# A program laid out step by step in one order, with one window geometry for all batches, in an attention and MoE kernel

## The chip, the cores and the metric

The kernel runs on one NeuronCore of a Trainium2 chip. Five engines work side by side, each through its own queue in program order: TensorE (PE) for matmuls, VectorE (DVE), ScalarE (ACT), GpSimd (POOL), and SyncE (SP), which only issues transfers. Transfers between HBM and on-chip memory (SBUF) run on the core's 16 DMA engines, whichever queue issued them. Matmul results go to PSUM, eight banks of 512 fp32 values on each of 128 partitions.

The metric is the device time of one execution in microseconds (us), as the median of several runs. Beside it stands one execution under the hardware profiler, with a time of its own, on which all readings of the trace rest.

## The reference

Two stages follow each other. The first is attention with B, H, S, D = 8, 8, 576, 64, as a sum of a coarse part (queries, keys and values averaged over groups of four tokens) and a local part (each query sees the keys less than four positions away):

```python
q_d, k_d, v_d = (x.reshape(B, H, S // 4, 4, D).mean(axis=3) for x in (q, k, v))
out_up = np.repeat(softmax(scale * q_d @ k_d.T) @ v_d, 4, axis=2)
mask = np.abs(pos[:, None] - pos[None, :]) < 4
out_local = softmax(np.where(mask, scale * q @ k.T, -1e9)) @ v
x = (out_up + out_local).transpose(0, 2, 1, 3).reshape(4608, 512)
```

The second is two dense layers on the 4608 tokens, with ELU between them:

```python
h = x @ w_in                                    # 512 -> 2048
g = np.where(h > 0, h, np.exp(np.minimum(h, 0)) - 1)
out = g @ w_out                                 # 2048 -> 512
```

## The kernel before

All matmuls take fp16 operands. The tokens of the dense layers are cut into nine blocks `t` of 512. A block's first layer (`mm1`, line 720) is 16 steps of four 128x512 matmuls, its second layer (`mm2`, line 740) 16 steps of four. Block 0 has its first layer cut into halves of 256 tokens (`mm1_part`, line 699), so that it can start on the first half. Between the layers each step has an exponential on ACT (line 724) and two DVE operations (lines 725 and 726).

Attention is done per batch `b` and pair of heads `j` (0 to 3); a batch gives 576 tokens, so block `t` needs batches up to about `t`. For a pair the steps are:

- **load**: `load_qk` and `load_v` on SP. For batches 0 and 1 (but the first pair) q and k are loaded by `load_cast` on POOL's queue, which converts to fp16 on the way. q and k lie as six tokens a partition on 96 partitions, two heads side by side. v comes as rows of 256 bytes.
- **cast**: `cast_qk`, `cast_v` on POOL, to fp16.
- **transposes** on PE (lines 324 and 329) into PSUM, and copies out (lines 359 and 366). From batch 3 on, k is turned by a transposing DMA (`flip`).
- **sums**: groups of four tokens, for q on POOL (lines 395, 397), for k on DVE (line 378).
- **scores** (lines 459, 472), exponentials on ACT (line 482), the mask on DVE (line 497), all in ten windows of 58 queries and 64 keys.
- **denominators** (line 519) of all four pairs and their reciprocals, spread over the partitions by matmuls and copies (lines 582, 592) for batches 0 to 2, and through DRAM (`spread_out`, `spread_in`) from batch 3 on.
- **outputs** (lines 603, 623), `normalise` on DVE (lines 667, 672), and the sum of both parts into the dense layers' input `xt` (line 684), nearly all on POOL.

Batch 0 has a geometry of its own: windows of 96 queries and 112 keys, a mask that is added by matmuls (line 423), sums of four tokens by matmuls (lines 340, 346), and outputs in two halves of the tokens. `keep` (line 759) are matmuls on zeros in the front that keep PE active.

The order is set by a time that is given to each step: `at(time, fn, *args)` collects the events, and they are emitted sorted by that time. The times stand in tables for the front (`F`), for batches 1 to 3 (`PLAN`), for later ones (`LATER`, `LAST`), and as straight lines for the matmuls of the dense layers (`MM1`, `MM2`). The tables put the loads of `w_in` (`load_wi`, line 172, four loads of 512 columns into one tile `WI`) behind the loads and casts of batch 0's v. PSUM tiles come from pools with turning buffers: two or three of two banks for transposes, scores and outputs, two of one bank for `hp`, two for the rest.

Of the kernel before, what the change touches and what calls it, by code (L numbers as in the profile page):

```python
# [19 lines left out]
QB, KW, NB, PAD = 96, 112, 6, 8  # L20
HB = 3 * QB
TPP = S // QB
# [5 lines left out]
RW = S + SD  # L28
KG, CG = 96, 24
# [6 lines left out]
I1 = 31  # L36


def _np_consts():

    f16 = np.float16
    off = np.arange(KW) - PAD
    m = np.zeros((KW, NB, QB), dtype=f16)
    for c in range(NB):
        for u in range(QB):
            ok = (np.abs(off - u) < 4) & (off + QB * c >= 0) & (off + QB * c < S)
            m[ok, c, u] = 1.0
    m = m.reshape(KW, S)
    neg = ((m - 1) * 30000).astype(f16)
    rs = np.zeros((QB, 3, SD), dtype=f16)  # L50
    for c in range(3):
        rs[np.arange(QB), c, (TPP * np.arange(QB) + 2 * c) // 4] = 0.25
    vr = np.zeros((KW, 32), dtype=f16)
    vr[PAD + np.arange(QB), np.arange(QB) // 4] = 0.25
    ind = np.zeros((KW, 190), dtype=f16)
    ind[:, I1] = 1.0
    ind[np.arange(KW) % 32 < CG, 63 + I1] = 1.0
    ind[:, 126:] = 1.0
    for n, z in enumerate((10, 5)):
        ind[:, 127 + 32 * n : 126 + 32 * n + z] = 0.0  # L60
    return np.eye(KW, dtype=f16), neg, rs.reshape(QB, 3 * SD), vr, ind


def _np_windows():
# [26 lines left out]
    return mask.reshape(128, WL), vr.reshape(128, 96), ind  # L91
# [12 lines left out]
def kernel(  # L104
# [11 lines left out]
    dr = ctx.enter_context(tc.tile_pool(name="dr", bufs=1, space=bass.MemoryType.DRAM))  # L116
    ctx.enter_context(nc.allow_low_precision("fp16 operands of TensorE"))
    ctx.enter_context(tc.manual_schedule())

    def const(a, name, queue):  # L120
        t = C[name] = sb.tile(list(a.shape), FP16, tag=name, bufs=1, name=name)
        queue.dma_start(out=t[:], in_=nc.inline_tensor(a, name=name + "c").ap())

    front = ctx.enter_context(ExitStack())
    ps = ctx.enter_context(tc.tile_pool(name="ps", bufs=1, space=bass.MemoryType.PSUM))
    fp = front.enter_context(tc.tile_pool(name="fp", bufs=1, space=bass.MemoryType.PSUM))
    late = {}

    def one(name, dt=FP32):
        return ps.tile([128, 512 if dt == FP32 else 1024], dt, tag="misc", bufs=2, name=name)  # L130

    turns = [0, 1, 2]

    def two(name, dt=FP32):

        turns.append(turns.pop(0))
        pool = fp if turns[-1] == 2 else ps
        return pool.tile([128, 1024 if dt == FP32 else 2048], dt, tag=f"two{turns[-1]}", bufs=1, name=name)

    def bank(tag, name):  # L140
        pool = late["ps"] if tag == "hp" else ps
        return pool.tile([128, 512], FP32, tag=tag, bufs=2, name=name)

    def close_front():
        front.close()
        turns.remove(2)
        late["ps"] = ctx.enter_context(
            tc.tile_pool(name="late", bufs=1, space=bass.MemoryType.PSUM)
        )

    def g2(ap, a, n):

        return _free(ap[:, a : a + 1], [[512, 2], [1, n]])
# [3 lines left out]

    id_np, neg_np, sums_np, vr_np, ind_np = _np_consts()
    mask_np, vr2_np, ind2_np = _np_windows()
    C = {}  # L160
    WI = sb.tile([128, DMC, DFF], FP16, tag="WI", bufs=1, name="WI")
    WO = sb.tile([128, FCN, DM], FP16, tag="WO", bufs=1, name="WO")
    KT = [sb.tile([128, S + 2 * KO], FP16, tag=f"kt{i}", bufs=1, name="kt") for i in range(4)]

    def w_in(dc, fc):

        a = 512 * (fc // 4) + fc % 4
        return WI[:, dc, a : a + 509 : 4]

    def load_wi(a, z):  # L170
        src = moe_w_in.rearrange("(c p) m -> p c m", p=128)[:, :, a:z]
        nc.gpsimd.dma_start(out=WI[:, :, a:z], in_=src)

    def load_wo(n):
        src = moe_w_out[512 * n : 512 * n + 512].rearrange("(p c) m -> p c m", c=4)
        nc.gpsimd.dma_start(out=WO[:, 4 * n : 4 * n + 4, :], in_=src)

    KD = [sb.tile([128, 2 * KG + 16], FP16, tag=f"kd{i}", bufs=1, name="kd") for i in range(4)]
    KE = [sb.tile([128, 192], FP16, tag=f"ke{i}", bufs=1, name="ke") for i in range(4)]
    QT = [sb.tile([128, S + 4], FP16, tag=f"qt{i}", bufs=1, name="qt") for i in range(4)]  # L180
    qk32, qk16, v32s, v16s = {}, {}, {}, {}
    st = {}

    def runs_of(src, b, j):

        a = src[b, 2 * j]
        return bass.AP(
            tensor=a.tensor, offset=a.offset, ap=[[TPP * D, QB], [S * D, 2], [1, TPP * D]]
        )

    def by_head(x):

        return x[:].rearrange("p c e d -> p (c e d)").rearrange("p (e n) -> p e n", e=2)

    def is_cast(b, j):

        return b < 2 and (b, j) != (0, 0)

    def load_cast(b, j):
        qk16[(b, j)] = []  # L200
        for src, name in ((q, "q16"), (k, "k16")):
            x = sb.tile([QB, NB, 2, D], FP16, tag=name, bufs=4, name=name)
            nc.gpsimd.dma_start(out=by_head(x), in_=runs_of(src, b, j))
            qk16[(b, j)].append(x)

    def load_qk(b, j, held=False):

        got = []
        for src, name in ((q, "q"), (k, "k")):
            a = src[b, 2 * j]  # L210
            t = sb.tile([QB, 2 * NB, D], FP32, tag=name + "32", bufs=3, name=name + "32")
            if held:
                nc.vector.memset(t[0:1, 0, 0:1], 0.0)
            runs_ = name == "q" or b < FLIP
            nc.sync.dma_start(
                out=t[:].rearrange("p (e r) d -> p e (r d)", e=2) if runs_ else t[:],
                in_=bass.AP(
                    tensor=a.tensor, offset=a.offset,
                    ap=[[TPP * D, QB], [S * D, 2], [1, TPP * D]] if runs_
                    else [[D, QB], [QB * D, 2 * NB], [1, D]],  # L220
                ),
            )
            got.append(t)
        qk32[(b, j)] = got

    AP_ = sb.tile([1, 1], FP16, tag="apart", bufs=1, name="apart")

    def apart(x):

        nc.gpsimd.tensor_copy(out=AP_[:], in_=x)  # L230

    def cast_qk(b, j, half=False):

        got = []
        for t, name in list(zip(qk32.pop((b, j)), ("q16", "k16")))[:: 1 if b < FLIP else -1]:
            x = sb.tile([QB, NB, 2, D], FP16, tag=name, bufs=4, name=name)
            src = t[:].rearrange("p (e c) d -> p c e d", e=2)
            if half:
                act(out=x[:, :, 0, :], in_=src[:, :, 0, :])
                dve(out=x[:, :, 1, :], in_=src[:, :, 1, :])  # L240
            else:
                nc.gpsimd.tensor_copy(out=x[:], in_=src)  # L242
                apart(x[0:1, 0, 0, 0:1])
            got.append(x)
        qk16[(b, j)] = got[:: 1 if b < FLIP else -1]

    V00 = sb.tile([KW, 2 * NB, D], FP32, tag="v32", bufs=3, name="v32")

    def load_v(b, j):

        a = v[b, 2 * j]
        if b:
            load_windows(b, j, a)
            return
        t = V00 if (b, j) == (0, 0) else sb.tile([KW, 2 * NB, D], FP32, tag="v32", bufs=3, name="v32")

        def part(p0, p1, i0, i1):
            nc.sync.dma_start(
                out=t[p0:p1, i0:i1, :],
                in_=bass.AP(  # L260
                    tensor=a.tensor, offset=a.offset + (QB * i0 - PAD + p0) * D,
                    ap=[[D, p1 - p0], [QB * D, i1 - i0], [1, D]],
                ),
            )

        if (b, j) == (0, 0):
            part(0, KW, 1, 2 * NB)
            part(PAD, KW, 0, 1)
        else:
            part(0, KW, 0, 2 * NB)  # L270
        v32s[(b, j)] = t

    def load_windows(b, j, a):

        t = sb.tile([128, 2 * WM, D], FP32, tag="v32", bufs=3, name="v32")
        if b == 1:
            nc.vector.memset(t[0:1, 1, 0:1], 0.0)

        def part(h, e, n=64, m0=0, m1=WM):
            nc.sync.dma_start(  # L280
                out=t[64 * h : 64 * h + n, WM * e + m0 : WM * e + m1, :],
                in_=bass.AP(
                    tensor=a.tensor, offset=a.offset + (WQ * h - 3 + S * e + 2 * WQ * m0) * D,
                    ap=[[D, n], [2 * WQ * D, m1 - m0], [1, D]],
                ),
            )
# [760 lines left out]
```

## Time and profile before

| | us |
|---|---|
| median of 3 runs | 352.03 (350.53 to 354.69) |
| span of the profiled execution | 355.1 |
| PE / DVE / ACT / POOL busy in it | 336.1 / 236.4 / 180.3 / 160.8 |
| `mm2` matmuls (line 740), 592 | 147.0 |
| `mm1` matmuls (line 720), 512 | 133.4 |
| `mm1` matmuls of block 0 (line 699), 128 of half the width | 17.3 |

How to read it: the span runs from the first to the last instruction. The busy time of an engine is the time in which at least one of its instructions ran; matmuls are pipelined, so one of them shows some 380 ns of its own while the next starts 216 ns after it. "PEclk" is the share of full speed that TensorE's clock was granted. A chain of waits lists, in order of time, the pieces of work that released each other up to the last instruction. Of DMA traffic the profile shows, by queue, packets, bytes, and the time that they took as a share of the 16 engines: q0 is what POOL issues, q1 what SP issues.

### The profile page before, as it was taken

The page shows a single profiled execution, that of the slowest core. Times are in us where ns is not written, and L with a number is a line of the kernel's source. Part 1 is how long each engine was busy: PE and PEld are TensorE (multiplying, and loading weights), DVE is VectorE, ACT ScalarE, POOL GpSimd, SP SyncE. Part 2 cuts the span into 40 slices and gives each one's busy share as a digit, 9 for nine tenths or more (in the row PEclk, how much of TensorE's full clock was granted, in tenths as well). Part 3 has the DMA queues.
Part 4 walks back from the last instruction along what each step waited for, and adds up shares of the span by engine and source line. Part 5 has one row for each costly group of instructions (what it writes and reads, how often), then busy time and mean ns, then how long its engine had stood idle before and what let it go on. Part 6 is the DMA issues. An engine that isn't in the chain of part 4 may idle for free.

```text
span 355.1 us, 10487 instructions
## 1 busy us (share of the span) xinstructions
PE 336.1 (95%) x4288; PEld 185.5 (52%) x4288; DVE 236.4 (67%) x466; ACT 180.3 (51%) x312; POOL 160.8 (45%) x298
## 2 busy tenths in 40 slices
PE   7993998799979999999999999999999999999996
PEld 3762885344545454545454555555455544444443
DVE  2334799566789877987697789768755855555510
ACT  4580587225755664466456645663553444444421
POOL 4464449279495834974397449855300500000000
PEclk9998799959999999999999999999999999999999
DMA  8999979997999698998979796943004010011012
GB/s 173 184 166 203 191 172 216 215 186 185 189 152 224 120 205 168 167 185 174 181 155 206 158 218 144 188 123 61 30 32 118 31 59 30 31 46 43 31 59 89
DMA packets 100304, 48.89 MB, mean 138 GB/s; under 512 B 81617, under 2 KB 95265, under 8 KB 100257
## 3 DMA queue, kind: packets, MB, share of 16 engines
q1 hardware_dynamic: 94417, 41.86, 57.8%
q0 software_dynamic: 5600, 6.26, 10.8%
q8 instruction: 33, 0.54, 0.7%
q10 hardware_dynamic: 240, 0.11, 0.2%
q14 instruction: 14, 0.11, 0.1%
HBM read 41.97 MB, written 9.55 MB: 145 GB/s over the span
## 4 chain that ended last, share of the span: by engine, by line
PE 72%; DMA 13%; DVE 6%; ACT 3%; issue 2%; POOL 2%; SPq 1%; DVEq 0%; POOLq 0%; ACTq 0%
PE op L740 31%; PE hp L720 28%; DMA v<-in_v_dram 6%; DMA rcb<-rd 3%; DMA WO<-in_moe_w_out_dram 3%; DVE ln L672 2%; PE sc L759 2%; PE tqk L329 2%; DMA rd<-rc 2%; PE lg L603 2%; DVE e L725 1%; PE sc L459 1%; ACT e L724 1%; DVE gt L726 1%; PE lg L623 1%
## 5 line engine op out<-in xcount | busy, mean ns | idle before, releaser
L740 PE MATMUL op<-WO,gt 128*128 128x512 f16 (+2 forms) x592 | 147.0, 377 | 1.0 <-DVE gt L726 0.6
L724 ACT ACTIVATE e<-hp 128x512 f16<-128x512 f32 x144 | 86.1, 599 | 110.5 <-PE hp L720 95.7
L720 PE MATMUL hp<-xt,WI 128*128 128x512 f16 x512 | 133.4, 384 | 0.7 <-DVE gt L726 0.5
L726 DVE SCALAR_TENSOR_TENSOR gt<-hp,e 128x512 f16<-128x512 f32 x144 | 99.6, 692 | 6.4
L725 DVE TENSOR_SCALAR e<-e 128x512 f16<-128x512 f16 x144 | 60.7, 421 | 58.1 <-ACT e L724 57.6
L740 PEld LDWEIGHTS <-gt 128*128 128x128 f16 x592 | 55.6, 98 | 62.8 <-issue 3.0
L720 PEld LDWEIGHTS <-WI 128*128 128x128 f16 x512 | 55.5, 115 | 49.6 <-issue 3.1
L684 POOL TENSOR_TENSOR xt<-ln 128x128 f16<-128x128 f16 (+7 forms) x55 | 36.7, 695 | 50.8 <-DVE ln L672 50.8
L482 ACT ACTIVATE pex<-sc 128x580 f16<-128x580 f32 (+1 forms) x56 | 30.2, 596 | 9.7 <-PE sc L472 9.7
L395 POOL TENSOR_TENSOR t<-qt 128x288 f32<-128x288 f16 x27 | 18.1, 671 | 36.8 <-ACT qt L359 36.8
L303 POOL CAST v<-v 128x640 f16<-128x640 f32 (+1 forms) x32 | 24.2, 756 | 21.1 <-DMA v<-in_v_dram 21.0
L746 ACT COPY os<-op 128x512 f32<-128x512 f32 (+2 forms) x37 | 21.4, 577 | 19.3 <-PE op L740 19.1
L378 DVE TENSOR_REDUCE ke<-kt 128x145 f16<-128x580 f16 x28 | 21.0, 751 | 2.4 <-ACT kt L366 2.4
L359 ACT COPY qt<-tqk 128x576 f16<-128x576 f16 x28 | 17.9, 638 | 8.5 <-PE tqk L329 6.7
L699 PE MATMUL hp<-xt,WI 128*128 128x256 f16 x128 | 17.3, 288 | 4.6 <-issue 4.6
L672 DVE TENSOR_TENSOR ln<-lg,rcb 128x580 f16<-128x580 f32 x28 | 21.1, 752 | 0.0
L242 POOL CAST q<-q 96x768 f16<-96x768 f32 x24 | 19.9, 828 | 0.0
L242 POOL CAST k<-k 96x768 f16<-96x768 f32 x24 | 19.8, 825 | 0.1
L699 PEld LDWEIGHTS <-WI 128*128 128x128 f16 x128 | 13.6, 118 | 5.8 <-issue 4.7
L497 DVE TENSOR_TENSOR pex<-pex,MASK 128x580 f16<-128x580 f16 x28 | 14.0, 500 | 3.8 <-ACT pex L482 3.6
L397 POOL TENSOR_TENSOR qd<-t 128x144 f16<-128x144 f32 x27 | 12.4, 461 | 2.1
L459 PEld LDWEIGHTS <-kt 64*64 64x64 f16 x560 | 7.0, 108 | 11.7 <-issue 8.8
(113 smaller groups left out, 271.6 us busy)
## 6 DMA issues: line engine op xcount, KB each, us to landing
out_dram<-os SPq DMA_DIRECT2D x35, 256.0 KB, 2.2
v<-in_v_dram SPq DMA_DIRECT2D x111, 80.0 KB, 4.6
q<-in_q_dram SPq DMA_DIRECT2D x25, 288.0 KB, 4.1
k<-in_k_dram SPq DMA_DIRECT2D x25, 288.0 KB, 5.1
rcb<-rd SPq DMA_DIRECT2D x10, 364.0 KB, 4.6
WI<-in_moe_w_in_dram POOLq DMA_DIRECT2D x4, 512.0 KB, 10.9
WO<-in_moe_w_out_dram POOLq DMA_DIRECT2D x4, 512.0 KB, 9.2
q<-in_q_dram POOLq DMA_DIRECT2D x7, 144.0 KB, 7.2
```

Source lines behind the costliest of these rows:

```text
L242: nc.gpsimd.tensor_copy(out=x[:], in_=src)
L303: nc.gpsimd.tensor_copy(out=v16[:], in_=v32[:].rearrange("p (e c) d -> p c e d", e=2))
L482: nc.scalar.activation(out=s["p"][:, :, a : a + n], in_=g2(sc, a, n), func=AF.Exp, scale=SCALE / 16 if a else SCALE,)
L672: nc.vector.tensor_tensor(out=ln[:, 0 : 2 * WL].rearrange("p (m h u) -> p m h u", h=2, u=WQ), in0=_free(lg[:, 0:1], [[WQ, WM], [512, 2], [ ...
L684: eng.tensor_tensor(out=xt(t)[:, j, t0 - TBLK * t : t1 - TBLK * t], in0=ln[:, a:z], in1=_rep4(ln[:, ga : ga + (z - a) // 4]), op=AB.add,)
L699: nc.tensor.matmul(FS[i][:, 256 * f : 256 * f + 256], w_in(dc, 2 * n + f), xts[0][:, dc, 256 * h : 256 * h + 256], start=(f == dc == 0), s ...
L720: nc.tensor.matmul(hp, w_in(dc, fc), xts[t][:, dc, :], start=(dc == 0), stop=(dc == DMC - 1),)
L724: nc.scalar.activation(out=e, in_=hp, func=AF.Exp)
L725: nc.vector.tensor_scalar(out=e, in0=e, scalar1=1.0, scalar2=-1.0, op0=AB.min, op1=AB.add)
L726: nc.vector.scalar_tensor_tensor(out=to, in0=hp, scalar=0.0, op0=AB.max, in1=e, op1=AB.add)
L740: nc.tensor.matmul(op_[:, a:z], gts[t][:, fc, 128 * tt : 128 * tt + 128], WO[:, fc, a:z], start=(fc == 0), stop=(fc == FCN - 1),)
L746: nc.scalar.copy(out=os_[:, a:z], in_=op_[:, a:z])
```

## The change

The program is written anew.

- **One geometry.** Batch 0 uses the windows of the later batches. Its mask, sums and token halves of its own go, and so do their constants (`NEG`, `R`, `SEL` and three more loads); what is left comes in one load, `con`.
- **Nine tokens a partition.** q and k are loaded as 9 tokens of one head on each of 128 partitions (rows of 2304 bytes; before: 1536). One transpose turns 64 partitions and 64 columns of one head, so a tensor takes 18 small transposes, two at a time in opposite corners of the array; before it was 6 or 12. From batch 3 on, k is loaded and turned by DMA as before.
- **Sums of four** are two additions of halves for q and k alike, each given to DVE or POOL.
- **PSUM by name.** Eight banks in four pairs; each step names its bank.
- **Whole blocks.** Block 0's first layer is made of 512-wide matmuls like the others. `WI` is two tiles, each loaded in two halves.
- **An order.** Each step is a word, `name.numbers`, the last number often the engine (0 ACT, 1 DVE, 2 POOL, 4 SP) or the bank; the words are carried out as they stand. Many steps get another engine than before: 44 of 64 `ad` (the sum into `xt`) are on DVE, 32 of 64 `s` on DVE, 12 of 82 casts on DVE and 6 on ACT, 10 of 144 `em` on POOL. Output pieces of the last 128 rows (384 and 128 columns) are interleaved, and the 128 columns are stored first.

The order up to the end of batch 0 reads as follows (`lx` load of q or k, `lv` load of v, `wi` load of `w_in`, `cx`/`cv` casts, `t` transposes, `e` copy out, `s` sums, `sc` scores, `x` exponentials, `mk` mask, `vs`/`vc` coarse v, `dn`/`rc` denominators, `sp`/`sy` spreading, `ne`/`fa` outputs, `n` normalise, `m` first layer, `w` second layer, `hv`/`hx` a write that holds a load back):

```diff
+ORDER = """
+id.0 zeros.0.1 lx.0.0.1.2 lx.0.0.0.4 zeros.2.1 warm.12.7 con.0 lx.1.0.0.4 lx.1.0.1.2 zeros.3.1 lv.0.0.1.4
+lx.0.0.3.2 zeros.1.1 lv.0.0.2.4 lx.0.0.2.2 lv.0.0.3.4 lx.1.0.3.2 lv.0.2.0.4 lx.1.0.2.2 lv.0.2.1.4 four.0.1
+wi.0.0.2 four.1.1 wi.0.1.2 lv.0.2.2.4 wi.1.0.2 cx.0.0.0.0 lv.0.2.3.4 t.0.0.1.4 t.0.0.0.5 lv.0.0.0.4
+e.0.0.1.4.0 wi.1.1.2 cx.1.0.0.1 e.0.0.0.5.0 s.0.0.1.1 lv.0.1.0.4 warm.2.7 t.1.0.1.6 t.1.0.0.7 s.0.0.0.1
+lv.0.1.1.4 e.1.0.1.6.0 lx.0.1.0.2 e.1.0.0.7.0 lv.0.1.2.4 s.1.0.1.1 warm.2.5 t.0.0.3.4 lv.0.1.3.4 s.1.0.0.1
+sc.0.1.0 e.0.0.3.4.0 lv.0.3.0.4 lx.1.1.0.2 sc.0.0.1 x.0.0.1.0 lv.0.3.1.4 s.0.0.3.1 warm.1.7 t.0.0.2.5
+x.0.0.0.1 mk.0.1.1 lv.0.3.2.4 e.0.0.2.5.0 mk.0.0.1 cv.0.2.2 lv.0.3.3.4 x.1.0.1.0 s.0.0.2.1 warm.6.7 t.1.0.3.6
+x.1.0.0.1 cv.0.0.2 vs.0.2.7 e.1.0.3.6.0 dn.0.0.2.4 lx.0.1.1.2 vs.0.0.5 s.1.0.3.1 lx.1.1.1.2 warm.2.3 t.1.0.2.6
+rc.0.0.2.4 sc.0.3.0 e.1.0.2.6.0 cv.0.1.1 sp.0.0.1 x.0.0.3.0 s.1.0.2.1 warm.1.4 vs.0.1.5 x.1.0.3.0 mk.0.3.1
+vc.0.0.5.0 warm.2.6 sc.0.2.0 sy.0.0.1.0 sp.0.1.2 x.0.0.2.0 ne.0.0.1 cv.0.3.1 lx.0.1.2.2 fa.0.0.1 x.1.0.2.0
+mk.0.2.1 warm.1.6 vs.0.3.7 sy.0.1.2.0 n.0.0.1 dn.0.2.4.6 vc.0.1.7.0 ne.0.1.0 hv.1.0.1 hv.1.1.1 hv.1.2.1
+hv.1.3.1 fa.0.1.0 lv.1.0.0.4 rc.0.2.4.6 ad.0.0.0.2 lv.1.0.1.4 n.0.1.0 warm.3.5 sp.0.2.2 lx.1.1.2.2 lv.1.0.2.4
+sp.0.3.1 ad.0.0.1.1 m.0.0.0.1.7 sy.0.2.2.0 lv.1.0.3.4 ad.0.1.0.1 ad.0.1.1.2 m.0.1.0.1.6 sy.0.3.1.0 lv.1.2.0.4
+m.0.0.1.2.7 ne.0.2.0 fa.0.2.0 lv.1.2.1.4 m.0.1.1.2.6 ne.0.3.1 n.0.2.0 lx.0.1.3.2 lv.1.2.2.4 fa.0.3.1
+lv.1.2.3.4 n.0.3.1 ad.0.2.0.2 lv.1.1.0.4 ad.0.2.1.1 lv.1.1.1.4 ad.0.3.0.1 ad.0.3.1.2 warm.15.5 m.0.0.2.3.7
...
+w.8.3.12.16.0.384.7 w.8.3.12.16.384.512.4 r.8.3.0.384.7.0 r.8.3.384.512.4.1 st.8.3.384.512 st.8.3.0.384
+"""
```

and the code that carries it out:

```diff
+    PB = [ps.tile([128, 1024], FP32, tag=f"pb{i}", bufs=1, name=f"pb{i}") for i in range(4)]
+    def bank(n):
+        return PB[n // 2][:, 512 * (n % 2) : 512 * (n % 2) + 512]
...
+    def load_x(x, b, j, eng):
+        a = (q, k)[x][b, 2 * j]
+        src = bass.AP(tensor=a.tensor, offset=a.offset, ap=[[NINE * D, 128], [1, NINE * D]])
+        if is_cast(b, j):
+            queues[eng].dma_start(out=nth((Q16, K16)[x], b, j)[:, 0:S], in_=src)
+            return
...
+    def load_wi(n, i, eng):
+        src = moe_w_in.rearrange("(c p) m -> p c m", p=128)
+        queues[eng].dma_start(
+            out=WI[n][:, 2 * i : 2 * i + 2, :], in_=src[:, 2 * i : 2 * i + 2, 1024 * n : 1024 * n + 1024]
+        )
...
+    def turn(x, b, j, p):
+        src, to = nth((Q16, K16)[x], b, j), bank(p).bitcast(FP16)
+        for c in range(NINE):
             for e in range(2):
+                r = heads(e)
+                nc.tensor.transpose(to[r, 64 * c : 64 * c + 64], src[r, 64 * c : 64 * c + 64], ID[r, r])
...
+    def sums(x, b, j, eng):
+        if x == 0:
+            src, n, to = QT[j][:, 0:S], SD, QD[j][:]
+        else:
+            src, n = KT[j][:, KO : KO + 2 * WL], 2 * WL // 4
+            to = KE[j][:, 0 : 32 * WM].rearrange("p (c u) -> p c u", u=32)[:, :, 0:WG]
+        t2 = T2[eng - 1][:, 0 : 2 * n]
+        at = src.rearrange("p (g f) -> p f g", f=2)
+        engines[eng].tensor_tensor(out=t2, in0=at[:, 0], in1=at[:, 1], op=AB.add)
...
+        engines[eng].tensor_tensor(out=to, in0=at[:, 0], in1=at[:, 1], op=AB.add)
...
+    def mm1(t, fc, d0, d1, p):
+        n, a = fc // 8, 512 * (fc % 8 // 4) + fc % 4
+        for dc in range(d0, d1):
             nc.tensor.matmul(
+                bank(p), WI[n][:, dc, a : a + 509 : 4], XT[t % 3][:, dc, :],
+                start=(dc == 0), stop=(dc == DMC - 1),
             )
...
+    for word in ORDER.split():
+        name, *numbers = word.split(".")
+        STEPS[name](*map(int, numbers))
```

More of the change, by code (lines that the diff above doesn't have):

```diff
@@ L116 @@
     dr = ctx.enter_context(tc.tile_pool(name="dr", bufs=1, space=bass.MemoryType.DRAM))
+    ps = ctx.enter_context(tc.tile_pool(name="ps", bufs=1, space=bass.MemoryType.PSUM))
     ctx.enter_context(nc.allow_low_precision("fp16 operands of TensorE"))
     ctx.enter_context(tc.manual_schedule())
[L120 to L138, printed above, removed]
@@ L162 @@
[L162 to L176, printed above, removed]
@@ new lines, in four, with warm @@
+    def four(n, eng):
+        if n == 0:
+            nc.vector.tensor_reduce(
+                out=I4[:], in_=_free(ID[:, 0:1], [[1, 16], [32, NPAIR]]), axis=AX.X, op=AB.add
+            )
+            return
+        copies[eng](
+            out=FOUR[:].rearrange("p (n e d) -> p n e d", e=2, d=64),
+            in_=_free(I4[:, 0:1], [[1, 8], [8, 2], [0, 64]]),
+        )
+    def warm(n, p):
+        for _ in range(n):
+            nc.tensor.matmul(bank(p), Z[:, 0:128], Z[:], start=True, stop=True)
@@ L228, in apart, with load_wo @@
+    def load_wo(n, eng):
+        src = moe_w_out[512 * n : 512 * n + 512].rearrange("(p c) m -> p c m", c=4)
+        queues[eng].dma_start(out=WO[n][:], in_=src)
     def apart(x):
         nc.gpsimd.tensor_copy(out=AP_[:], in_=x)
[L232 to L245, printed above, removed]
@@ L568, in spread_half @@
[L568 to L579 removed]
+        nc.sync.dma_start(out=rd[:], in_=RC[b % 2][:])
```

1085 lines of the change are left out of this document (400 added, 685 removed).

## The prediction

> **What bounds the kernel now.** I read the page's slices first, then stretches of the span, then the chain of waits. Busy tenths in 40 slices of 8.9 us:
>
> ```profile
> span 355.1 us, 10487 instructions
> PE   7993998799979999999999999999999999999996
> DVE  2334799566789877987697789768755855555510
> PEclk9998799959999999999999999999999999999999
> DMA  8999979997999698998979796943004010011012
> ```
>
> PE is full from the thirteenth slice on, and the DMA engines are nearly full until 240 us. So there are two regimes. The stretches below (PE, PEld, DVE, ACT, POOL busy with counts, clock, DMA share, GB/s) give them numbers:
>
> ```profile
> 30.00:40.00 10.00, 5.72 (x68) 4.18 (x68) 4.01 (x6) 1.08 (x2) 5.84 (x10) 0.66 1.29 206
> 76.10:80.00 3.90, 3.90 (x13) 1.43 (x11) 2.91 (x5) 1.78 (x3) 3.38 (x6) 0.50 0.81 180
> 86.00:116.00 30.00, 27.25 (x463) 15.49 (x462) 24.95 (x46) 18.23 (x32) 20.22 (x39) 1.00 1.07 187
> 183.20:217.00 33.80, 33.80 (x469) 17.66 (x467) 27.41 (x50) 18.87 (x33) 20.85 (x42) 1.00 0.94 181
> ```
>
> 183.2 to 217.0 is one whole block: 128 dense matmuls (64 of each layer, the rows of lines 720 and 740 below) and 341 small ones of attention. Four dense matmuls follow each other in 0.86 us, 0.2162 each:
>
> ```profile
> 278.68 0.97 PE op L740 x4
> 279.65 0.86 PE hp L720 x4
> ```
>
> So the dense part is 128 x 0.2162 = 27.7 us, and 33.8 - 27.7 = 6.1 us for 341 small matmuls is 18 ns each, with the 0.11 us that the first group after attention costs more (0.97). The same two prices on 86 to 116 us, with 48 + 35 = 83 dense and 380 small ones:
>
> ```profile
> 0.00:80.00 80.00, 2.33 (x5) 0.83 (x6) 0.90 1.05 190
> 86.00:116.00 30.00, 12.28 (x48) 5.04 (x49) 1.00 1.07 187
> ...
> 0.00:80.00 80.00, 8.96 (x28) 2.73 (x28) 0.90 1.05 190
> 86.00:116.00 30.00, 8.46 (x35) 2.97 (x33) 1.00 1.07 187
> ```
>
> (line 720 above the gap, line 740 below). 17.9 + 6.8 = 24.7 us of work in 30: 5.3 us are lost there. And up to 80 us only 5 + 28 dense matmuls are done beside block 0's first layer, 64 in full width: 97 of 1152. The front is where time can be won; after 116 us PE has no gap to give.
>
> The chain of waits says why the front is long, and the timeline where block 0's first layer begins in earnest:
>
> ```profile
> 25.70 11.13 DMA v<-in_v_dram
> 36.84 8.99 DMA v<-in_v_dram
> 55.32 10.15 DMA WO<-in_moe_w_out_dram
> 34.28 1.02 PE L699 MATMUL hp<-xt,WI 128*128 128x256 f16 x4 [4.65 <-issue]
> 40.06 4.56 PE L699 MATMUL hp<-xt,WI 128*128 128x256 f16 x40
> ```
>
> **The change: the front.** It loads the same q, k, v and weights, less a quarter of a megabyte of constants, but POOL issues all of `w_in` right behind batch 0's q and k, before v of pairs 1 and 3 (before: behind the casts of v). DMA between 18.3 and 34.2 us, packets, MB and share of 16 engines, and v alone between 13 and 18:
>
> ```profile
> q0 software_dynamic: 2488, 2.37, 92.3%
> q1 hardware_dynamic: 2268, 0.56, 25.9%
> ...
> q1 hardware_dynamic: 2851, 0.72, 72.5%
> ```
>
> Where `w_in` runs, v gets 0.56 MB in 15.9 us, 35 GB/s, against 144 alone. So `w_in` pushes v back; but the engines are full either way, and what decides is the last of batch 0's v and `w_in`. In the old order that was `w_in` (PE resumes at 34.28, and then it reads all of it), with some six v loads of batch 1 ahead: 6 x 320 rows x 29 ns (25.9% of 16 engines over 15.9 us, by 2268) / 16 = 3.5 us. Without them v of pair 3 lands at about 31 us. The bounds: 22 us if v is served before `w_in`, 34 if behind three casts of batch 1 too.
>
> From there DVE's order is what counts: the casts of v of pairs 1 and 3 stand in it ahead of a mask, all four `n` and the reciprocals, so the whole queue waits for that landing. Behind it come, from these rows:
>
> ```profile
> L726 DVE SCALAR_TENSOR_TENSOR gt<-hp,e 128x512 f16<-128x512 f32 x144 | 99.6, 692 | 6.4
> L725 DVE TENSOR_SCALAR e<-e 128x512 f16<-128x512 f16 x144 | 60.7, 421 | 58.1 <-ACT e L724 57.6
> L672 DVE TENSOR_TENSOR ln<-lg,rcb 128x580 f16<-128x580 f32 x28 | 21.1, 752 | 0.0
> L667 DVE TENSOR_TENSOR ln<-lg,rcb 128x144 f16<-128x144 f32 x28 | 8.4, 300 | 4.4 <-PE lg L623 2.6 <-DMA rcb<-rd 1.8
> L684 DVE TENSOR_TENSOR xt<-ln 128x448 f16<-128x448 f16 x1 | 0.6, 626 | 0.0
> L497 DVE TENSOR_TENSOR pex<-pex,MASK 128x580 f16<-128x580 f16 x28 | 14.0, 500 | 3.8 <-ACT pex L482 3.6
> L525 DVE RECIPROCAL rc<-den 128x91 f16<-128x91 f32 x7 | 5.1, 728 | 1.1 <-PE den L519 1.0
> L303 POOL CAST v<-v 128x640 f16<-128x640 f32 x28 | 20.8, 744 | 12.3 <-DMA v<-in_v_dram 12.3
> L759 PE MATMUL sc<-Z 128*128 128x512 f16 x20 | 7.6, 515 | 1.2 <-DVE v L766 1.2
> ```
>
> a cast (0.7, as on POOL), the mask 0.5, four normalisations of 1.05, the reciprocal 0.7, four additions (0.15 and 0.7, twice): 7.8 us, to 39. On PE fifteen matmuls on zeros stand in the way of the second half of the first step: 3.2 us at full clock, 6 at the half clock that the last row shows in the start (7.6 us for 20). I take 41 us for the start of block 0's main run, against 40.06: no gain there.
>
> From that start to the first step of block 1 PE has 60 + 40 dense matmuls (21.6 us), 688 small ones (12.4) and 8 on zeros (1.7): 35.7 us. DVE has 16 sums at 0.69, 13 minima at 0.42, 5 casts of v, 4 of k or q (0.5, scaled from the cast row), 4 copies out (0.7, as the similar ones), 4 normalisations, 5 additions, 4 masks, 3 sums of four, a reciprocal and small writes: 11.1 + 5.5 + 3.5 + 2 + 3 + 4.2 + 2.7 + 2 + 1.7 + 0.7 + 0.5 = 36.9. A sum of four is two additions of 290 and 145 elements, 0.57 us at the 1.3 ns an element of the 448-element row. Two full queues that feed each other in order don't run without gaps; I add 3 us. Block 1 begins at 79.5.
>
> What is done by then? 64 + 40 = 104 dense matmuls, 7 more than before at 80 (1.5 us), two pairs of transposes and one of scores more (1.4), and before ran at half clock to 80.8 (the row of 76.1 to 80; 0.4). So the change at 79.5 stands where before stood at 83.3: **3.8 us won**. The pieces whose disappearance pays for this are block 0's half-width matmuls (17.3 us for what 64 full ones do in 13.8, the rows of the small table above) and the wait of 4.65 us for all of `w_in`, less the v that now comes later.
>
> **The change: from there on.** Of the 5.3 us lost between 86 and 116 I take half back (2.6), since a step can now use any of four PSUM banks, and DVE is the engine that was 83% busy there: bounds 0 and 5.3. Transposes of q become 18 small ones in place of 6. The nearest rows of the chain are
>
> ```profile
> 8.93 0.45 PE tq L324 x12
> 82.08 0.51 PE tqk L329 x12
> 84.32 0.28 PE sc L459 x20
> ```
>
> 0.26 us for the six of q (0.51 holds q and k). 18 small ones cost 0.25 at the 14 ns of the third row, 0.38 at 21 (twelve transposes of the first row, whose next twelve start 0.25 us later): 0 to 0.12 us more, over some 24 tensors 0 to 3. The order has 40 separate runs of attention between dense matmuls from block 1 on, some twenty fewer than the old plan's timed events make, at 0.11 us each: 2 us less. I take 0 for both together, -2 to +3. The Trainium skill, "TensorE: Matmul & The Clock Gate", section "Wait — 56ns, not 53.3ns?", says that matmuls never start less than about 25 ns apart; by it the 18 would be 0.45 us and the sum an estimated 4 us worse. The row of scores, 14 ns apart in four corners of the array, disagrees, and the row decides.
>
> The tail: the 384 columns of the last rows are stored behind the 128, one issue (0.4 us) later. DVE's longer list is hidden under PE as long as DVE stays below it (rival below); the loads are no more than before and PE's lead over them is kept.
>
> Sum: 355.1 - 3.8 - 2.6 + 0 + 0.4 = 349.1 us of profiled span. The runs shown have a median of 352.03 against 355.1 in the profile, 0.9914: **346 us**.
>
> **Rivals.** *v is served first (faster).* The v loads get through beside `w_in`: the row of 13 to 18 us shows what SP can move, and the long rows of `w_in` are only 64 for each engine. Against it stand the 35 GB/s. Then v is there at 22 us, the main run starts when `w_in`'s first half and the chain allow, about 33, and block 1 at 71: 8.5 us more, 338 x 0.9914 = 335.
>
> *DVE takes PE's place (slower).* Additions and casts moved from POOL raise DVE's 27.41 us a block by 5.5 additions (2.8), 1.5 casts (0.9), less 0.7 for the sums of k: 30.4 of 33.8. That alone fits. But DVE is slowed beside POOL: with POOL idle after 300 us the minimum takes 295 ns,
>
> ```profile
> L725 DVE TENSOR_SCALAR e<-e x23: 295/295/295, 300.2 to 338.2; 128x512 f16<-128x512 f16 x23
> ```
>
> and 421 in the mean. If each of the 13 operations a block that DVE gets in new form (additions, halves of sums) waits 0.4 us for a POOL instruction, it is 35.6 us: 1.8 us a block over PE, from 33.8 on. Six blocks with attention: +10.8, 360 x 0.9914 = 357. For it: DVE was 83% busy where PE lost 5.3 us. Against it: POOL itself gets less to do. The Trainium skill has this as a rule ("SBUF — State Buffer", section "Who interferes with whom"): a DVE instruction with two inputs in SBUF contends with a GpSimd instruction that reads SBUF. The additions moved are of that kind; no row here shows an addition slowed.
>
> *The front comes later (nothing won).* v lands at 34 and PE's zeros run at half clock: start at 46, block 1 at 84.5; the gain of 3.8 becomes a loss of 1, and with half the later gain the time is 354 x 0.9914 = 351.
>
> **Numbers.** Forecast 0.40, v first 0.18, DVE 0.25, late front 0.17. A measurement of this kernel tells about 1% (348.5 to 355.5 is no change). Faster: 0.18, three quarters of the forecast's case (343 to 350) 0.30, none of the rest: 0.48. Same: 0.08 of the forecast and 0.13 of the late front: 0.21. Slower: 0.31. Range: from the first rival, 335, to the DVE case with a front 3 us late, 360.
>
> **What would show it.** Right: the main run of block 0 starts at 39 to 43 us, block 1 at 77 to 82, and PE is full from there. v of pair 3 is waited for by DVE until about 31 us. Wrong: DVE over 32 us a block with PE waiting for it; a start under 36 or over 45; half clock beyond 50 us; PE gaps of over a microsecond after 120 us.

## The result and the profile after

| | before | changed |
|---|---|---|
| median, us | 351.8 (4 runs) | 427.8 (424.28 to 429.68, 4 runs) |
| ratio to before | 1 | 1.217 (95%: 1.207 to 1.228) |
| span of the profiled execution | 355.1 | 427.3 |

The changed kernel is slower by a fifth, against a forecast of 346 us and a range that ended at 360. Two executions of one of these kernels differ by up to 3%, so a difference of a few us between two single profiles below shows little by itself. The slices of the changed kernel, 10.7 us each:

```profile
span 427.3 us, 11118 instructions
PE   6369777887788878887788799788988987888895
DVE  4235566597679668955797688676635666245300
PEclk9855999998999999999999999999999999999999
DMA  8994594589589699799786424031003100010022
```

Before, PE stood at 9 from the thirteenth slice to the last. Now it stands at 7 and 8 nearly all the way, even towards the end, where POOL has nothing left, DMA is nearly idle and only dense matmuls are in flight. DVE does not stand at 9 there either: no engine is full. That is the look of engines that wait for each other in turn. The list of PE's waits names the pair (engine and line that wait, engine and line waited for, us in total, times, longest):

```profile
PE pb L641 <- DVE gt L657: 18.2, 21, 1.9
PE pb L524 <- POOL v L446: 11.0, 1, 11.0
PE pb L641 <- ACT e L650: 10.0, 18, 0.7
PE pb L674 <- DVE gt L657: 6.2, 8, 1.4
```

In the kernel before, the first and the last of these rows (there lines 720, 740 and 726) were next to nothing:

```profile
PE op L740 <- DVE gt L726: 0.6, 1, 0.6
PE hp L720 <- DVE gt L726: 0.5, 2, 0.3
```

From the lists of DVE and ACT of the changed kernel:

```profile
DVE gt L657 <- PE pb L641: 20.1, 25, 1.8
ACT e L650 <- DVE gt L657: 37.7, 25, 3.0
```

L641 and L674 are the matmuls of the two layers, L650 the exponential, L654 the minimum, L657 the sum. By the data a sum needs the minimum and the matmuls of its own step, and the minimum has already waited for those matmuls. Here 25 sums wait for matmuls of the first layer nevertheless, and 25 exponentials for a sum. The timeline shows whose (start, duration, and in brackets the idle time before it and what ended it):

```profile
326.42 0.28 DVE L654 TENSOR_SCALAR e<-e 128x512 f16<-128x512 f16 x1
326.56 1.02 PE L674 MATMUL pb<-WO,gt 128*128 128x512 f16 x4 [0.95 <-DVE gt L657]
327.42 1.03 PE L641 MATMUL pb<-xt,WI 128*128 128x512 f16 x4
328.49 0.69 DVE L657 SCALAR_TENSOR_TENSOR gt<-pb,e 128x512 f16<-128x512 f32 x1 [1.78 <-PE pb L641]
329.15 1.03 PE L641 MATMUL pb<-xt,WI 128*128 128x512 f16 x4
329.21 0.60 ACT L650 ACTIVATE e<-pb 128x512 f16<-128x512 f32 x1 [2.96 <-DVE gt L657]
```

The words of this place are `m.6.13.0.4.5`, `m.6.14.0.4.4`, `em.6.13.1 es.6.13.5`, `ex.6.14.4`. The minimum of step 13 is done at 326.70. Its sum reads bank 5 and all that it needs is there. It starts at 328.49, 0.04 us after the matmuls of step 14, which write bank 4. Then the exponential of step 14, in bank 4, starts at the end of that sum's read of bank 5. Banks 4 and 5 are the two halves of one tile, `PB[2]`.

The stretches from block 1's first matmul on (us, then PE, PEld, DVE, ACT, POOL busy with counts, clock, DMA share, GB/s) give the size; the first pair is the changed kernel, the second the kernel before:

```profile
96.20:200.00 103.80, 85.44 (x1238) 43.73 (x1238) 75.97 (x149) 49.95 (x90) 60.71 (x113) 0.98 0.97 178
200.00:427.30 227.30, 190.88 (x2035) 94.60 (x2033) 128.49 (x262) 84.27 (x150) 48.66 (x73) 1.00 0.27 67
```

```profile
76.20:200.00 123.80, 120.05 (x1702) 63.08 (x1700) 96.74 (x175) 71.66 (x126) 79.85 (x153) 0.98 0.94 179
200.00:355.10 155.10, 152.16 (x1403) 76.84 (x1400) 97.11 (x186) 69.26 (x119) 40.98 (x75) 1.00 0.32 79
```

331.1 us from block 1 on, of which PE is idle for 331.1 - 85.4 - 190.9 = 54.8; before, 278.9 with 6.7. Block 1 itself starts at 96.2 in place of 76.2.

### The profile page after: what moved, and what is told of

Its sections match the earlier page's. It is cut to its first block, busy times and chain, and to the rows that moved or that the text cites. A ratio compares the mean times of both kernels' runs of the same rounds, so it can differ in the third digit from the quotient of the medians.

```text
span 427.3 us, 11118 instructions
## 1 busy us (share of the span) xinstructions
PE 347.8 (81%) x4607; PEld 176.4 (41%) x4607; DVE 258.3 (60%) x546; ACT 177.5 (42%) x313; POOL 150.7 (35%) x250
## 4 chain that ended last, share of the span: by engine, by line
PE 51%; DVE 19%; ACT 11%; DMA 6%; issue 5%; POOL 4%; SPq 2%; DVEq 0%; ACTq 0%; POOLq 0%
PE pb L641 22%; PE pb L674 19%; DVE gt L657 11%; ACT e L650 7%; DMA v<-in_v_dram 5%; POOL e L654 2%; DVE e L654 2%; PE pb L456 2%; PE pb L365 2%; SPq L398 2%; DVE xt L631 1%; PE pb L591 1%; PE pb L524 1%; DVE ln L620 1%; ACT qt L465 1%
## 5 line engine op out<-in xcount | busy, mean ns | idle before, releaser
L641 PE MATMUL pb<-xt,WI 128*128 128x512 f16 x576 | 144.7, 385 | 34.3 <-DVE gt L657 18.2
L674 PE MATMUL pb<-WO,gt 128*128 128x512 f16 (+2 forms) x592 | 141.0, 375 | 15.6 <-DVE gt L657 6.2
L650 ACT ACTIVATE e<-pb 128x512 f16<-128x512 f32 x144 | 83.2, 597 | 136.6 <-PE pb L641 71.2
L657 DVE SCALAR_TENSOR_TENSOR gt<-pb,e 128x512 f16<-128x512 f32 x144 | 99.0, 690 | 48.1 <-PE pb L641 20.1
L641 PEld LDWEIGHTS <-WI 128*128 128x128 f16 x576 | 64.4, 114 | 95.6 <-issue 44.1
L674 PEld LDWEIGHTS <-gt 128*128 128x128 f16 x592 | 55.5, 98 | 82.5 <-issue 22.9
L654 DVE TENSOR_SCALAR e<-e 128x512 f16<-128x512 f16 x134 | 42.4, 318 | 56.7 <-ACT e L650 56.4
L683 ACT COPY os<-pb 128x512 f32<-128x512 f32 (+1 forms) x36 | 21.0, 582 | 49.5 <-PE pb L674 28.9
L631 POOL TENSOR_TENSOR xt<-ln 128x512 f16<-128x512 f16 (+7 forms) x20 | 14.8, 747 | 53.5 <-DVE ln L620 47.0
L654 POOL TENSOR_SCALAR e<-e 128x512 f16<-128x512 f16 x10 | 19.6, 1955 | 32.9 <-ACT e L650 32.9
L631 DVE TENSOR_TENSOR xt<-ln 128x448 f16<-128x448 f16 (+7 forms) x44 | 30.3, 720 | 0.1
L446 POOL CAST v<-v 128x640 f16<-128x640 f32 x23 | 18.7, 812 | 30.0 <-PE pb L591 16.0
L507 ACT ACTIVATE pn<-pb 128x580 f16<-128x580 f32 x32 | 20.6, 657 | 9.8 <-PE pb L500 8.9
L620 DVE TENSOR_TENSOR ln<-pb,rcb 128x580 f16<-128x580 f32 x32 | 24.0, 750 | 0.0
L478 POOL TENSOR_TENSOR t<-qt 128x288 f32<-128x288 f16 x19 | 13.3, 699 | 22.7 <-ACT qt L465 18.6
```

The lines of the kernel that those rows point to most:

```text
L478: engines[eng].tensor_tensor(out=t2, in0=at[:, 0], in1=at[:, 1], op=AB.add)
L620: nc.vector.tensor_tensor(out=ln[:, 0 : 2 * WL].rearrange("p (m h u) -> p m h u", h=2, u=WQ), in0=_free(lg[:, 0:1], [[WQ, WM], [512, 2], [ ...
L631: engines[eng].tensor_tensor(out=XT[t % 3][:, j, t0 - TBLK * t : t1 - TBLK * t].rearrange("p (u f) -> p u f", f=4), in0=ln[:, a:z].rearran ...
L641: nc.tensor.matmul(bank(p), WI[n][:, dc, a : a + 509 : 4], XT[t % 3][:, dc, :], start=(dc == 0), stop=(dc == DMC - 1),)
L650: nc.scalar.activation(out=e_of(t, fc), in_=bank(p), func=AF.Exp)
L654: engines[eng].tensor_scalar(out=e, in0=e, scalar1=1.0, scalar2=-1.0, op0=AB.min, op1=AB.add)
```

## The experiments

**Banks apart.** Theory A says that a wait covers a whole tile of two banks. Three kernels test it: the changed one with four banks, or two, as tiles of their own, and the kernel before with its two `hp` banks made halves of one tile.

```diff
-    PB = [ps.tile([128, 1024], FP32, tag=f"pb{i}", bufs=1, name=f"pb{i}") for i in range(4)]
+    PB = [ps.tile([128, 1024], FP32, tag=f"pb{i}", bufs=1, name=f"pb{i}") if i not in SPLIT else None for i in range(4)]
+    BK = {i: ps.tile([128, 512], FP32, tag=f"bk{i}", bufs=1, name=f"bk{i}") for i in range(8) if i // 2 in SPLIT}
     def bank(n):
+        if n in BK:
+            return BK[n][:]
```

`SPLIT` is (2, 3):

> The changed kernel with banks 4 to 7 as four tiles of one bank each, in place of two tiles of two banks; every step keeps its bank, its engine and its place in the order. (The two spreadings of batch 0 that span banks 4 and 5 are copied out by two instructions.) Theory A, a wait is kept for each tile and so a step on one bank waits for steps on its neighbour: PE's idle time beyond the first 40 us (61 us) goes for the most part, span 345 to 366 us, and the rows 'PE pb <- DVE gt' and 'PE pb <- ACT e' in the list of waits shrink from 28 us to under 6. Theory B, DVE contends with POOL and its queue is too long: nothing changes on DVE, span stays at 405 to 430 us. Theory C, the order itself leaves gaps (three banks turn too fast for the chain exponential, minimum, sum): span 380 to 410 us.

`SPLIT` is (3,):

> The changed kernel with only banks 6 and 7 as tiles of their own; banks 4 and 5 stay one tile. Theory A: part of the gain, since two of the four banks still wait for each other: span 375 to 400 us. Theories B and C: as the changed kernel, 415 to 430 us.

The kernel before, where `bank("hp", name)` gave a tile of one bank in turn:

```diff
+        late["hp"], late["n"] = late["ps"].tile([128, 1024], FP32, tag="hp", bufs=1, name="hp"), 0
...
+        if tag == "hp":
+            late["n"] += 1
+            a = 512 * (late["n"] % 2)
+            return late["hp"][:, a : a + 512]
```

> The kernel before with its two turning banks for the first layer as the two halves of one tile; nothing else moves. Theory A: mm1 writes one half while the other is read, so each step waits for the other's sum: the chain 0.86 + 0.6 + 0.4 + 0.7 us and latencies are no longer beside the next step's matmuls; with an mm2 group in between to fill, 0.5 to 1 us for each of 128 steps, span 400 to 480 us. Theories B and C: unchanged, 350 to 356 us.

Measured medians: 377.27 us with both pairs apart (ratio to before 1.071, with a 95% interval of 1.064 to 1.078), 410.27 with one pair apart (1.162, 1.151 to 1.174), and the kernel before on one tile 474.74 (1.345, 1.338 to 1.351). The same steps on the same engines in the same order (but for the two copies that were cut in two), and 50.5 us go when the halves are named as tiles; the kernel before loses 122 us when they are not. Theories B and C fall as the main cause. A's sizes were too hopeful twice: spans of 374 against 345 to 366, 411 against 375 to 400. With one pair apart both sorts of bank stand side by side in one kernel (`pb` is the pair that is still one tile, `bk` a bank apart), and the waits stand at the pair:

```profile
PE pb L649 <- DVE gt L665: 13.1, 14, 1.3
PE bk L649 <- DVE gt L665: 2.9, 2, 2.7
```

The same stretch of the order, one step earlier, with both pairs apart (here the exponential is L658, the minimum L662, the sum L665, the matmuls L649 and L682):

```profile
285.36 0.60 ACT L658 ACTIVATE e<-bk 128x512 f16<-128x512 f32 x1 [0.23 <-PE bk L649]
285.99 0.29 DVE L662 TENSOR_SCALAR e<-e 128x512 f16<-128x512 f16 x1 [0.58 <-ACT e L658]
286.02 1.03 PE L649 MATMUL bk<-xt,WI 128*128 128x512 f16 x4
286.32 0.69 DVE L665 SCALAR_TENSOR_TENSOR gt<-bk,e 128x512 f16<-128x512 f32 x1
286.89 1.03 PE L682 MATMUL bk<-WO,gt 128*128 128x512 f16 x4
287.09 0.60 ACT L658 ACTIVATE e<-bk 128x512 f16<-128x512 f32 x1 [1.13 <-PE bk L649]
```

The sum of step 12 starts 0.04 us after its minimum, while the matmuls of step 13 run, and PE's groups follow each other in 0.87 us. In the kernel before on one tile, one row holds most of the loss (it was the 0.5 us above):

```profile
PE hp L724 <- DVE gt L730: 95.0, 109, 2.4
```

109 of its groups wait for the sum of the other half, 0.9 us each. Two pages of the Trainium skill bear on this. The Trainium skill, "Perfetto Trace Analysis", section "Matmuls", advises to let independent groups rotate through banks so that the read of one overlaps the matmuls of the next; the changed kernel does rotate, and in these runs the overlap comes only when each bank is a tile. The Trainium skill, "PSUM — Partial Sum Buffer", section "PSUM bank collisions raise a hardware error", asks for a guard by bank (and quadrant). The waits of the changed kernel are wider than that: 328.49 waits for another bank.

**What stays.** With the banks apart the medians are still 24 us from the kernel before (377.27 against 353.04). The stretches and the waits of that kernel:

```profile
83.90:200.00 116.10, 103.22 (x1589) 53.71 (x1587) 98.46 (x181) 58.48 (x104) 73.05 (x135) 0.94 1.04 188
200.00:373.80 173.80, 167.63 (x1704) 85.24 (x1692) 109.68 (x230) 78.11 (x136) 36.37 (x52) 1.00 0.26 70
```

```profile
PE bk L528 <- POOL v L450: 11.9, 1, 11.9
PE pb L495 <- DVE ln L628: 6.0, 4, 4.9
PE bk L649 <- DVE gt L665: 3.3, 2, 2.2
```

From block 1 on PE is idle for 289.9 - 103.2 - 167.6 = 19.1 us, and the clock of 0.94 over 116 us costs some 7 more (before: 0.98 over 124 us, some 2.5). The chain of waits puts the longest holes, as idle stretches of PE are called here, down to the loads of the spread reciprocals:

```profile
137.28 7.84 DMA rcb<-rd
182.57 6.37 DMA rcb<-rd
```

Twelve kernels follow; eleven are this one with one edit or two. The first moves those loads ahead in SP's queue:

```diff
-so.3
-lv.4.3.0.4
-...
-si.3.0 si.3.1
+so.3 si.3.0 si.3.1
+lv.4.3.0.4
+...
```

> The kernel with the banks apart (377 us), and the two loads that spread the reciprocals of batches 3, 4 and 5 (rcb) stand in SP's queue right behind the store they read, in place of behind eight, seven and four other loads and a store. Theory A, the late rcb sets the two longest holes of PE after 140 us (3.2 us around 146, 4.9 us at 185, each with 3.4 to 6.8 us of half clock behind it): rcb lands 4 to 6 us earlier, both holes go, span 374 becomes 362 to 368. Theory B, DVE's queue is full there anyway (9.9 of 10 us busy at 150 to 160): 371 to 374, no more than 3 us.

The second gives all sums into `xt` back to POOL (`ad.b.j.t.1` becomes `ad.b.j.t.2`, 44 words), the third does both:

> The kernel with the banks apart (377 us), and all 64 sums into xt on POOL, as in the kernel before, in place of 44 on DVE. Theory A, DVE took PE's place (9.8 of 10 us busy from 80 to 130 us): 31 us less on DVE, PE's holes between 80 and 125 us (5 us and a half clock of 3.4) go, span 374 becomes 362 to 369. Theory B, POOL's casts and sums already stand in a queue (8.6 to 9.2 of 10 us busy at 80 to 90 and 110 to 120), xt is later by the queue's length: 378 to 395.

> Both edits of the two runs before this one together. If the two holes have causes of their own the gains add: by theory A of both, 350 to 360. If one chain carries both, the sum is that of the better one.

The next moves the words `wi.0.0.2 wi.0.1.2 wi.1.0.2 wi.1.1.2` behind `lv.0.3.3.4`, the last load of v of batch 0, which puts them behind the cast `cv.0.2.2`:

> The kernel with the banks apart (377 us), and the four loads of w_in stand in POOL's queue behind the cast of v of pair 2, in place of ahead of it. Theory A, w_in's traffic is what holds batch 0's v back (v of pair 2 lands at 24.5 us, PE waits 11.9 us for it, and runs at half clock until 29): v lands by 13 to 17 us, the wait shrinks to 2 to 5 us, the main run of block 0 starts at 33 to 37 in place of 41 us, span 374 becomes 366 to 370. Theory B, the engines are full either way and w_in is now the last: v earlier, w_in at 30 to 33 us, start 38 to 41 us, span 371 to 374.

Two take work away, apart and together:

```diff
-        else:
-            part(0, 64, 0, WM)
+        elif b < 2:
+            part(0, 64, 0, WM)
+        else:
+            part(0, 64, 0, 1)
...
+        n = WL if b == 0 else WQ
...
+        if t >= 3 and eng == 1:
+            t1 = min(t1, t0 + 64)
```

> The kernel with the banks apart (377 us, span 374), and v of batches 2 to 7 loaded to a fifth (one of five windows; the rest of the tile keeps what an earlier batch left, so the outputs of those batches are not the reference's; casts and matmuls are the same). 81 to 16 KB a load, about 7.7 MB less traffic between 40 and 220 us. Theory A, PE's holes between 84 and 200 us come from loads that land late as a set (moving rcb ahead only made k late): rcb and k land 2 to 4 us earlier, the holes around 146 and 185 go with their half clock, span 352 to 362. Theory B, DVE's queue is the bound there: span 369 to 374.

> The kernel with the banks apart (377 us, span 374), and less work on DVE: the mask of batches 1 to 7 covers 58 of 290 columns, and DVE's sums into xt cover 64 tokens each from block 3 on (so those outputs are not the reference's; the number of instructions is the same). Some 25 us less on DVE. Theory A (loads): span 369 to 374. Theory B (DVE): the holes shrink, span 358 to 367.

> Both cuts together (outputs as in those two). Theory A: as y1 alone within 2 us. Theory B: as y2 alone within 2 us. If both hold each other up, below either: 345 to 352.

One puts the ten minima of POOL on DVE (`em.t.f.2` becomes `em.t.f.1`), and one replaces `so` and `si` of batches 3 to 5 by `sp` and `sy`:

> The kernel with the banks apart (377 us, span 374), and all 144 minima on DVE, in place of 10 on POOL, where one takes 1.9 us against 0.3 to 0.4 on DVE. Theory C, a minimum on POOL holds its bank 1.5 us longer and PE's next step in that bank with it: 0.5 to 1 us for each of the ten, span 365 to 370. Against it: PE has other steps to do meanwhile, span 373 to 375.

> The kernel with the banks apart (377 us, span 374), and the reciprocals of batches 3, 4 and 5 spread by matmuls and copies, as those of batches 0 to 2, in place of through DRAM. Theory A, late rcb loads are the cause of the two holes and everything behind them is in time: the holes at 146 and 185 us go, block 1 to the end takes 278 to 282 us in place of 290 (PE does 24 spreadings of 0.19 us more). Theory B, all loads of that stretch are late together (as y1 showed: 283 with v cut): the hole moves to the next load or cast, 286 to 290.

Two keep PE busy in the front with the words `warm.45.7` ahead of `vs.0.2.7`, or, on the order with `w_in` behind v, `warm.4.7` there and `warm.24.4` ahead of `vs.0.1.5`:

> The kernel with the banks apart (377 us, span 374) and 45 more matmuls on zeros, 9.7 us at full clock, at the place where PE waits 11.9 us for v of pair 2 of batch 0. Theory A, the hole of PE is what costs it its clock (15.6 to 29.3 us at half in that kernel, up to 46 us in its relatives), and the half clock is what makes their block 1 start anywhere between 83 and 89 us: full clock from 25 us on, main run at 38 to 41, block 1 at 80 to 83, span 368 to 372. Theory B, the front waits for tokens and DVE, not for PE: block 1 at 83 to 85, span 372 to 376.

> As the run with w_in behind v (378 us, block 1 at 87.5 at half clock until 41.5), with 4 and 24 more matmuls on zeros where it waited 3 and 6 us for v. Theory A: no half clock, main run at 36 to 38, block 1 at 80 to 83, span 366 to 371. Theory B: as that run, 376 to 381.

And the kernel before with `w_in` in four tiles:

```diff
-    WI = sb.tile([128, DMC, DFF], FP16, tag="WI", bufs=1, name="WI")
+    WI = [sb.tile([128, DMC, 512], FP16, tag=f"WI{i}", bufs=1, name="WI") for i in range(4)]
```

> The kernel before with w_in in four tiles, one for each of its four loads, in place of one tile; nothing else moves. Theory A, a wait is kept for each tile (or for the stretch of addresses that a slice spans): PE's wait of 4.65 us until 34.28, when the last of the four loads has landed, goes, since the parts it does there need the first load only (landed at 23.1) and later the second (27.7); the half clock of 33 to 39.8 us goes with it. The main run at 40 us still waits for the tokens of pairs 1 and 3, so of the 4.65 us at most the matmuls done early are won: 1 to 4 us, time 348 to 351. Rival: the wait is for the tokens, not for w_in, and nothing changes: 351 to 354.

Measured; block 1 is its first matmul, and PE idle is the stretch from there to the end less PE's busy time in it (some 4 us of it, 3 in the last row, is the tail behind PE's last matmul):

| kernel | median, us | block 1 at | block 1 to end | PE idle in it |
|---|---|---|---|---|
| banks apart | 377.27 | 83.9 | 289.9 | 19.1 |
| spread loads ahead | 382.57 | 86.3 | 294.0 | 24.2 |
| sums into xt on POOL | 380.37 | 84.4 | 294.2 | 22.8 |
| both | 385.36 | 83.1 | 298.3 | 29.1 |
| w_in behind v | 377.65 | 87.5 | 293.8 | 20.8 |
| v cut | 370.98 | 87.4 | 282.9 | 16.1 |
| DVE cut | 377.91 | 85.8 | 290.7 | 22.7 |
| v and DVE cut | 369.54 | 89.4 | 281.4 | 13.5 |
| minima on DVE | 380.44 | 88.0 | 289.0 | 19.0 |
| spread by matmul | 380.03 | 85.9 | 292.5 | 17.9 |
| zeros while waiting | 376.98 | 87.1 | 289.7 | 20.3 |
| w_in behind v, zeros | 375.72 | 86.6 | 290.6 | 17.8 |
| before, w_in apart | 353.48 | 72.7 | 280.7 | 8.3 |

(With `w_in` behind v the two executions took 372.25 and 383.05 us, with v and DVE cut 366.53 and 372.55; these two medians decide nothing, and the columns behind them are of the longer one.) Up to block 1 the first two rows and the spreading by matmul are the same program, yet it starts at 83.9, 86.3 and 85.9. So differences of 2 to 3 us in that column say nothing; block 1 to the end tells more.

What follows, in the order of the table:

- *Spread loads ahead*: a miss for both theories. At the first hole the reciprocals are in time, and one of 4.4 us at 149 to 153 opens for another load:

```profile
142.92 6.31 DMA k<-in_k_dram
149.29 0.82 POOL k L439
```

  The second hole stays, 4.1 us at 189 (4.9 at 185 with the banks apart). There the reciprocals land at 192.1, no earlier than without the edit (188.9, with block 1 2.4 us earlier): SP issues their load only when the store it reads has landed, and the store itself starts at 182.0:

```profile
182.03 3.54 DMA rd<-rc
186.23 5.90 DMA rcb<-rd
```

- *Sums on POOL, DVE cut, minima on DVE*: none wins anything. 17 us less work on DVE (261.7 to 244.6 busy) leaves 377.9. So DVE's amount of work is not the bound, though it is over 97% busy in some stretches of 10 us. The sums are as theory B had them (a span of 378.6 in 378 to 395); the minima came out above both forecasts (377.0).
- *Both*, spread loads and sums: 8 us slower, the sum of the two losses (5.3 and 3.1), where gains had been expected.
- *`w_in` behind v*: v of pair 2 comes earlier, so PE's wait of 11.9 us for it shrinks to 1.2, with 3.1 more for pair 0. But v of pair 3 is cast at 31.5, as late as in the changed kernel (31.05), and PE waits 6.0 us for it. The main run starts at 44.1, later than either theory had it.
- *v cut*: 7 us from block 1 on, with the clock of its stretch at 0.98 in place of 0.94. Cutting v, alone or with DVE's work, is the only edit that helps there; all others stand between 289.0 and 298.3. A had asked for 12 to 22 us of span; the span fell by 3.5, into B's range, since block 1 starts 3.5 us later here, and the median by 6.3. B's reason, DVE's queue, is out by the cut of DVE's work:

```profile
87.40:200.00 112.60, 102.90 (x1605) 53.70 (x1604) 100.82 (x190) 62.27 (x110) 75.69 (x141) 0.98 0.79 159
```

- *Spread by matmul*: the long hole at 185 shrinks to 1.7 us (at 195), but the spreadings keep PE and ACT busy (PE 274.6 in place of 270.9 us from block 1 on), and it ends later. B's pattern, beyond its size.
- *Zeros*: the wait for v is filled, and nothing comes of it: the main run starts at 43.3 and block 1 at 87.1, later than either theory had it. On the order with `w_in` behind v it is 43.3 and 86.6, B's pattern; there the second group of zeros stands ahead of pair 1, the wait is at pair 3, and 3.8 us of it stay.
- *Before, w_in apart*: PE's wait of 4.65 us is gone and block 1 starts 3.5 us earlier in its one profile, but the time is the same (ratio 1.0006, 0.996 to 1.005). So the wait for all of `w_in` in the kernel before was a wait for a tile too, and taking it away wins nothing that can be measured.

No version beats the kernel before. What makes the other 24 us is settled in part only: the loads that come late as a set carry some 7 of them, by the cut of v; the rest did not go with any edit, and which step would have to move stays open. One rival was not tested: banks 0 to 3, of the scores and outputs, and `xt` are still tiles that several steps write in parts.

## Why the prediction was wrong

**The step that failed** is in the part "from there on": "since a step can now use any of four PSUM banks". I counted it as a gain of 2.6 us. Four names are not four banks when two of them share a tile, and the price is 53.5 us of span (427.3 - 373.8): 12.3 ahead of block 1, 41.2 behind it. "PE is full from there", under "What would show it", was the ground on which every later term stood, and the one rival that put it in doubt did so by DVE's queue, not by the banks. The part ahead of block 1 is rough: three kernels with the banks apart that are the same up to there begin it between 83.9 and 86.3. The diff showed the tile: `PB` of 1024 columns and `bank(n)` as a slice of it. And the profile of before held the hint: PE waited at 29.6 to 34.3 us for all of `w_in`, one tile with four loads, and I read that as a matter of the front alone.

The rest of the miss, 373.8 - 349.1 = 24.7 us, is 4.4 in the front (block 1 at 83.9 against 79.5) and 20.3 from there on (289.9 against 269.6): PE's holes and the half clock behind them, which I priced at nothing beyond the half of the 5.3 us that I left in. The work on PE itself was sized about right: 289.9 less some 15 of holes ahead of the tail and 7 of half clock is 268.

**The front, by its steps.** In the changed kernel v of pair 3 is cast at 31.05, after a wait for its load, as forecast (31); the fifteen matmuls on zeros take 3.41 us (forecast 3.2):

```profile
31.05 0.82 DVE L446 CAST v<-v 128x640 f16<-128x640 f32 x1 [0.54 <-DMA v<-in_v_dram]
41.91 3.41 PE L365 MATMUL pb<-Z 128*128 128x512 f16 x15
45.16 1.24 PE L641 MATMUL pb<-xt,WI 128*128 128x512 f16 x5
```

With `w_in` behind v it is cast at 31.5 in that kernel's profile, which fits the argument that the engines are full either way. The main run starts at 45.16 against 41, just over the bound I had named. With the banks apart it starts where I said:

```profile
40.93 1.24 PE L649 MATMUL bk<-xt,WI 128*128 128x512 f16 x5
```

That agreement is partly luck. Five other kernels with the banks apart, the same up to this point, start their main run at 43.1 to 47.7 in their profiles, so the 45.16 need not be an effect of the tiles either. And the wait that I put on DVE's queue is on PE's: it stands at the sums of v of pair 2 for 11.0 us (second row of the waits above), with all of PE's work queued behind. I had followed pair 3 and not asked what stands in front of it. The gain of 3.8 us did not come. Whether it would have counted is open: with `w_in` apart the kernel before is 3.5 us ahead at block 1 and not at the end. My reading, not tested, is that a gain in the front is worth its size only if the loads of the later batches come earlier too.

**The small terms.** 36 transposes take 0.76 us, so the 18 of a tensor 0.38, my upper bound, and below the 0.45 that I set aside:

```profile
208.32 0.76 PE pb L456 x36
```

Some sums of the prediction don't come out; none of them makes the miss. 41, DVE's 36.9 and 3 make 80.9, not 79.5 (79.7 with PE's 35.7). The first rival's 349.1 less 8.5 is 340.6, a time of 338 and not 335. The late front, 5 us later with half of the 2.6 lost, is 355.4, a time of 352 and not 351.

**The rivals.** v was not served first: pair 3 is cast at 31.05, not at 22. The slower rival had the sign, not the cause. DVE is busy for 258 of 427 us, its minimum takes 318 ns in the mean (421 before), and with the banks apart taking work off DVE won nothing. Its place in the list kept the chance of "slower" at 0.31; its price, bounded by one engine's queue, kept the range at 360. The late front (block 1 at 84.5) describes the front with the banks apart, 83.9, but the half of the later gain that it kept did not come.

## What to carry to other kernels

Ask of each buffer that a change merges or names anew which object carries its waits: two halves of one tile that are used in turn by different engines ran as one buffer here, and in a loop of matmul, exponential and sum that cost 50 us of 428, and 122 of 475 when the kernel before was built so. The sign of it in a profile is a wait that the data don't need (a sum that waits for the next step's matmul) while no engine is full. And an order laid out ahead step by step is only as good as its model of the loads: moving two loads ahead opened a hole at another load and left the next hole where it was.

## What the runs showed that I had not expected

PE can be busy without a gap and still run at half clock. With the 45 matmuls on zeros it is busy for 9.8 us at full clock, waits 1.4 and 0.6 us, and then works for 10 us without idle time, in small matmuls for the most part, at half:

```profile
14.00:23.80 9.80, 9.80 (x47) 4.31 (x46) 0.77 (x2) 0.64 (x1) 0.00 (x0) 1.00 1.14 204
27.00:37.00 10.00, 10.00 (x199) 5.59 (x197) 5.76 (x15) 5.25 (x10) 3.06 (x5) 0.50 0.45 76
```

The Trainium skill, "TensorE: Matmul & The Clock Gate", section "What's actually happening", has the clock come back after one busy window of about 3.4 us. Here the clock stays at half for 10 us, nearly three such windows, with PE busy throughout, so busy in the profile's sense is not enough to bring it back. What it depends on was not tested.

And the minimum on 128x512 is six times as long on POOL as on DVE (rows of the changed kernel):

```profile
L654 DVE TENSOR_SCALAR e<-e 128x512 f16<-128x512 f16 x134 | 42.4, 318 | 56.7 <-ACT e L650 56.4
L654 POOL TENSOR_SCALAR e<-e 128x512 f16<-128x512 f16 x10 | 19.6, 1955 | 32.9 <-ACT e L650 32.9
```
